# Slot packing and the slot-softmax multiply on GpSimd, and another order of the first loads, in a fused attention and maxout-FFN kernel

## The chip, the cores and the metric

The kernel runs on one core of a Trainium2 chip. The metric is device time in microseconds of one execution; lower is better. A profiled execution gives a trace of every instruction on the engines: TensorE (PE in the profile, its weight loads PEld), VectorE (DVE), ScalarE (ACT), GpSimd (POOL) and SyncE (SP), and of the DMA transfers.

## The reference

Eight batches of eight heads, 576 tokens, head size 64, 32 memory slots; then an FFN over the 4608 tokens with model size 512 and inner size 768.

```python
def _attn_ref(q, k, v, phi):
    a = phi - np.max(phi, axis=2, keepdims=True)
    a = np.exp(a)
    a = a / (np.sum(a, axis=2, keepdims=True) + 1e-09)      # over the tokens
    k_m = np.einsum('bhsm,bhsd->bhmd', a, k)                # slot keys
    v_m = np.einsum('bhsm,bhsd->bhmd', a, v)                # slot values
    scores = 1.0 / np.sqrt(q.shape[-1]) * np.matmul(q, k_m.transpose(0, 1, 3, 2))
    scores = scores - np.max(scores, axis=-1, keepdims=True)
    attn = np.exp(scores)
    attn = attn / (np.sum(attn, axis=-1, keepdims=True) + 1e-09)   # over the slots
    return np.matmul(attn, v_m)

def _moe_ref(x, w1, w2, w3, w_out):       # x: the heads side by side, [4608, 512]
    h = np.maximum(np.maximum(x @ w1, x @ w2), x @ w3)
    return h @ w_out
```

All inputs and the output are float32 in memory.

## The kernel before

**Order.** Nothing is scheduled by the framework (`tc.manual_schedule()`). The kernel ends in one long written list of words such as `B@2`, each a step of one batch, and `issue` turns a word into instructions. Every engine executes its own instructions in the order of this list, and waits where data or a buffer is missing. A `!` swaps the engine that evicts a result from PSUM (ScalarE or VectorE, by the table `EVAC`).

**Loads.** Loads that convert to bf16 are issued from GpSimd's queue: `load_kv` (k and v), `load_q`, `load_w` (w1, w2, w3) and `load_wo` (w_out); phi, which stays float32, goes from SyncE's queue for batch 0 and from GpSimd's for the others. In the list, `H0` and `H2` are the two halves of k of batch 0, `H1` and `H3` the two halves of v, `L0` to `L3` are phi, k, v and q, `Y0` to `Y3` are w1, w2, w3 and w_out. Inputs have two buffers each; `kvos` are two tiles with three parts for k, v and ones, the ones written once by VectorE at the start.

**Attention of a batch.** `E` takes the exponential of phi on ScalarE. `B` (`att_kv`, matmul at L209) multiplies it with k, v and the ones: 72 small multiplies, eight of them side by side in the array, each with 192 columns (64 of k, 64 of v, 64 ones, of which one column is the sum over the tokens). For batch 1 it is done in two parts, `B0` (k and ones) and `B1` (v). `N` divides by that sum on VectorE, `K` transposes the result by TensorE. `Q` transposes q on VectorE, `S` forms the scores and their exponentials e2. The softmax over the slots is done on VectorE with 32x32 transposes: `a` (L310) transposes e2 to t, `s` (L318) sums over the slots, `c` (L327) takes the reciprocals, `m` (`att_mul`, L332) multiplies, `X` (`att_back`, L340) transposes back into attn. Each of these five exists for two groups g = 0 and 1 of heads.

**FFN.** The slot values are multiplied into the weights, so that the FFN runs on attn directly: `D` (`fold`, L363) forms, for a batch, the product of v_m with w1 - w3 and w2 - w3 (`D0`, `D1`, `D2`, `D4`) and with w3·w_out (`D3`). The max of three products is written as w3 plus a max of differences; w3·w_out is formed once at the start (`W` transposes w3, `O0` to `O3` multiply with w_out at L161), and `V` (`w_diff`, L182) subtracts w3 from w1 and w2 in place. Batch 0 is folded before that subtraction, with a second term (`kvtn`), in four groups of columns given by `FIRST`. `F` (`ffn1`, L389) multiplies attn with a folded weight: the even ones take w1 and are evicted with a relu to h1, the odd ones take w2 and end in the max at L402 on VectorE (hT). `T` (`ffn2`, L420, L429, L438 and at the end L461, L469) forms 128 rows of the output, evicts them (L141) and stores them from SyncE's queue.

**PSUM** is used through one pool of four tiles, each for any step. `Z` issues multiplies of zeros that keep TensorE running at the start.

The steps around the change at the start stand in the list as

```
H3@0 I@0 H2@0 H0@0 H1@0 E@0 Z38@0 B@0 N@0 Z3@0 K@0 L3@0 Q0@0 Q1@0 Z7@0 S@0 a0@0 Y2@0
Y3@0 a1@0 s0@0 s1@0 c1@0 Z6@0 W0@0 W2@0 Y0@0 Y1@0 W1@0 Z10@0 O1@0 O0@0 O2@0 m1@0 D1@0!
c0@0 m0@0 X0@0 D0@0 O3@0 L0@1 L1@1 L3@1 L2@1 X1@0 F8@0 F0@0 V0@0 F2@0 D4@0! D2@0 L0@2
V2@0 F10@0 F6@0 F11@0 F9@0 E@1 F4@0 F3@0 F1@0 F7@0 F5@0 D3@0 B0@1 T3@0 N0@1 Q0@1 K0@1!
```

and the functions that the change touches are these:

Of the kernel before, what the change touches and what calls it, by code (L numbers as in the profile page):

```python
# [15 lines left out]
def kernel(  # L16
# [102 lines left out]
    warm = const.tile([P, BANK], BF16, name="warm")  # L119
    nc.vector.memset(warm, 0.0)  # L120
    nc.vector.memset(kvos[0][:, 2], 1.0)
    nc.vector.memset(kvos[1][:, 2], 1.0)

    def warm_up(n):
# [44 lines left out]

    w12 = w_sb[:, :, 0:2].rearrange("p j i f -> p j (i f)")  # L170

    FIRST = {0: (0, 384), 1: (384, 768), 2: (768, 1152), 4: (1152, 1536)}

    def columns(b, n):
        return FIRST[n] if b == 0 else (n * BANK, (n + 1) * BANK)

    def w_diff(n):

        c, end = n * BANK, (n + 1) * BANK
        while c < end:  # L180
# [6 lines left out]
            )  # L187
            c = e

    st = {}  # L190

    def att_exp(b, js=slice(0, NP)):
        s = st.setdefault(b, {})
        if "e" not in s:
            s["e"] = work.tile([P, NP, NC, M], BF16, name="e")
        nc.scalar.activation(out=s["e"][:, js], in_=loaded[b]["ph"][:, js], func=AF.Exp)  # L196

    def att_kv(b, part=None):
        s = st[b]
        kvp = acc_pool.tile([P, NG, BANK], FP32, name="kvp", tag="acc")  # L200
        s["kvp", part] = kvp
        kv = loaded[b]["kv"]
        cols = {None: slice(0, 3), 0: slice(0, 3, 2), 1: slice(1, 2)}[part]
        nd = {None: 3 * D, 0: 2 * D, 1: D}[part]
        for c in range(NC):
            for j in range(NP):
                for a in range(NG):
                    r = slice(HP * a, HP * (a + 1))
                    nc.tensor.matmul(  # L209
                        kvp[M * j : M * (j + 1), a, 0:nd],  # L210
                        lhsT=s["e"][r, j, c, :],
                        rhs=kv[r, cols, j, c, :],
                        start=(c == 0),
                        stop=(c == NC - 1),
                        tile_position=(HP * a, M * j),
                    )
# [57 lines left out]
    attns = {}  # L274

    def att_score(b):
# [22 lines left out]
        for a in range(NG):  # L299
# [4 lines left out]
                scale=0.125,  # L304
            )

    def att_t(b, g):
        s = st[b]
        t = s["t", g] = work.tile([P, S // HP, R, 2], BF16, name="t", tag=f"t{g}")
        nc.vector.transpose(  # L310
            out=t.rearrange("p n r e -> p (n r e)").bitcast(FP32),
            in_=s["e2"][:, g].bitcast(FP32),
        )
# [15 lines left out]
    def att_mul(b, g):  # L329
        s = st[b]  # L330
        t = s["t", g]
        nc.vector.tensor_tensor(  # L332
            out=t,
            in0=t,
            in1=s["sm", g].unsqueeze(2).to_broadcast([P, S // HP, R, 2]),
            op=ALU.mult,
        )

    def att_back(b, g):
        nc.vector.transpose(  # L340
            out=attns[b // 2][:, g, (b % 2) * S : (b % 2 + 1) * S].bitcast(FP32),
            in_=st[b]["t", g].rearrange("p n r e -> p (n r e)").bitcast(FP32),
        )
# [140 lines left out]
    def issue(b, n, swap):  # L484

        i = int(n[1:]) if len(n) > 1 else None
        {
            "I": lambda: make_identity(nc, ident),
            "Y": lambda: load_w(i) if i < 3 else load_wo(),
            "L": lambda: load_ph(b) if i == 0 else load_q(b) if i == 3 else load_kv(b, i - 1),  # L490
            "H": lambda: load_kv(b, i % 2, halves[i // 2]),
            "E": lambda: [att_exp(b, h) for h in (halves if b == 0 else [slice(0, NP)])],
            "B": lambda: att_kv(b, i),
            "N": lambda: att_kv_norm(b, i),
            "K": lambda: att_kv_t(b, swap, i),
            "Q": lambda: att_q(b, i),
            "S": lambda: att_score(b),
            "a": lambda: att_t(b, i),
            "s": lambda: att_sum(b, i),
            "c": lambda: att_rec(b, i),  # L500
            "m": lambda: att_mul(b, i),
            "X": lambda: att_back(b, i),
            "D": lambda: fold(b, i, swap),
            "F": lambda: ffn1(b, i, swap),
            "T": lambda: ffn2(b, i, swap),
            "W": lambda: w3_t(i, swap),
            "O": lambda: w3_o(i, swap),
            "V": lambda: w_diff(i),
            "Z": lambda: warm_up(i),
        }[n[0]]()  # L510


    for w in """
        H3@0 I@0 H2@0 H0@0 H1@0 E@0 Z38@0 B@0 N@0 Z3@0 K@0 L3@0 Q0@0 Q1@0 Z7@0 S@0 a0@0 Y2@0
        Y3@0 a1@0 s0@0 s1@0 c1@0 Z6@0 W0@0 W2@0 Y0@0 Y1@0 W1@0 Z10@0 O1@0 O0@0 O2@0 m1@0 D1@0!
        c0@0 m0@0 X0@0 D0@0 O3@0 L0@1 L1@1 L3@1 L2@1 X1@0 F8@0 F0@0 V0@0 F2@0 D4@0! D2@0 L0@2
        V2@0 F10@0 F6@0 F11@0 F9@0 E@1 F4@0 F3@0 F1@0 F7@0 F5@0 D3@0 B0@1 T3@0 N0@1 Q0@1 K0@1!
        T1@0 Q1@1 S@1 V1@0 E@2 L1@2 B1@1 L0@3 N1@1 a0@1 a1@1 K1@1 T2@0! s0@1 s1@1 D0@1 c0@1
        D2@1 c1@1 m0@1 D1@1! m1@1 T0@0! L2@2 X0@1 X1@1 F4@1! F5@1 L3@2 L2@3 F10@1 L1@3 F11@1
        F8@1 F0@1 F2@1 F3@1 L3@3 F6@1 F9@1 F1@1 E@3 F7@1 B@2 D3@1 N@2 Q1@2 Q0@2 T3@1 K@2! T2@1!  # L520
        S@2 a0@2 T1@1 T0@1! L0@4 D0@2 s0@2 L2@4 D1@2! a1@2 c0@2 m0@2 s1@2 c1@2 m1@2 X1@2 T4@1!
        X0@2 D3@2 L1@4 B@3 L0@5 N@3 D2@2 F6@2! Q1@3 F10@2 F2@2 F8@2 Q0@3 K@3! F3@2 F0@2 F7@2
        S@3 F1@2 F11@2 F4@2 F9@2 F5@2 E@4 D0@3 L1@5 a1@3 a0@3 D1@3! T0@2! T1@2 s0@3 D3@3 s1@3
        c1@3 m1@3 X1@3 D2@3 B@4 c0@3 E@5 T2@2! L2@5 L3@5 m0@3 X0@3 L3@4 F2@3 N@4 F0@3 F8@3
        F10@3 F1@3 F6@3 F3@3 K@4 F4@3 F7@3 F9@3 F5@3 D0@4 B@5 N@5 D1@4! F11@3 T3@2 Q0@5 K@5
        T4@3! Q1@5 S@5 L0@6 Q0@4 Q1@4 a1@5 a0@5 T1@3 s1@5 D0@5 S@4 T0@3! L0@7 s0@5 c0@5 a0@4
        c1@5 m0@5 D3@5 a1@4 m1@5 D1@5! D2@5 E@6 s1@4 X1@5 c1@4 T2@3! X0@5 s0@4 L2@7 T3@3 m1@4
        L1@7 F4@5 F0@5 F2@5 L3@7 c0@4 X1@4 m0@4 F1@5 F5@5 F3@5 X0@4 E@7 F10@5 F8@5 F9@5 D3@4
        B@7 N@7 D2@4 F11@5 F6@5 F4@4 F10@4 F8@4 Q0@7 L3@6 Q1@7 K@7 F7@5 L1@6 F0@4 Q1@6 S@7 a1@7
        L2@6 F11@4 s1@7 F5@4 a0@7 T1@5 s0@7 F6@4 c1@7 T3@5 c0@7 m0@7 F2@4 F1@4 F3@4 D1@7! D3@7  # L530
        B@6 m1@7 N@6 D2@7 T2@5! X1@7 Q0@6 K@6 F9@4 F7@4 S@6 T4@5! D0@7 a0@6 s0@6 X0@7 D0@6 a1@6
        s1@6 c1@6 m1@6 X1@6 T3@4 D3@6 D2@6 c0@6 D1@6! T0@5! T1@4 F6@7 F2@7 F0@7 m0@6 X0@6 F3@7
        F4@6 F8@6 F7@7 F9@6 F6@6 F2@6 F1@7 F5@6 F4@7 F5@7 F0@6 F7@6 F10@6 F8@7 F10@7 F9@7 F1@6
        F11@7 T2@4! F11@6 T2@7! F3@6 T1@7 T0@7! T2@6! T0@6! T3@6 T1@6 T0@4! T4@7! T3@7
    """.split():
        n, b = w.rstrip("!").split("@")
        issue(int(b), n, w.endswith("!"))
# [30 lines left out]
```

## Time and profile before

| | |
|---|---|
| median of 5 runs | 167.0 us (166.63 to 167.36) |
| the profiled execution | 167.07 us, its span 165.3 us |
| TensorE busy | 155.7 us, 94% of the span |
| VectorE, ScalarE, GpSimd busy | 104.6, 98.7, 28.3 us |
| granted TensorE clock | full in all 40 slices |
| DMA | 31.77 MB, mean 192 GB/s |

The profile is one execution. Its page gives the busy time of each engine, 40 equal slices of the span (a digit is the busy share in tenths), the chain of work that ended last, and groups of instructions by source line with their mean duration and the idle time ahead of them with what ended it. The trace also answers questions by time: a timeline of one engine, the busy time of a stretch, the landing time of each transfer (the time from its issue until its data is there). Busy time of GpSimd here counts the issue of loads, of which there are 37.

### The profile page before, as it was taken

What the parts mean: (1) busy time and instruction counts of PE and PEld (TensorE: products, weight loads), DVE (VectorE), ACT (ScalarE), POOL (GpSimd) and SP (SyncE); (2) the same over time, 40 slices, a digit from 0 to 9 for tenths busy, and PEclk for the clock granted to TensorE, in tenths of its full rate; (3) what the DMA queues carried; (4) which work ended last, traced back from release to release, by engine and by line L of the source; (5) the groups of instructions that cost most, each with busy time, mean ns of one, the idle gap of its engine ahead of it and who ended that gap; (6) DMA issues with size and microseconds to landing.
All of it is one profiled execution on the core that took longest, in us unless ns stands there. A gap on an engine that the chain in (4) does not pass through costs nothing.

```text
span 165.3 us, 4664 instructions
## 1 busy us (share of the span) xinstructions
PE 155.7 (94%) x2006; PEld 87.6 (53%) x2024; DVE 104.6 (63%) x196; ACT 98.7 (60%) x148; POOL 28.3 (17%) x43
## 2 busy tenths in 40 slices
PE   7998799999799999999999999999999999999990
PEld 2443434673367444755674437765544677544450
DVE  5406882597786766999399798979999076510010
ACT  4200216964598459997953899984859867124220
POOL 7952110050600500610104600000000000000000
PEclk9999999999999999999999999999999999999999
DMA  5999999999999999999999999993113200124342
GB/s 159 177 202 211 189 209 239 250 207 280 316 240 254 204 246 324 261 280 209 261 237 347 233 261 234 261 198 96 69 67 127 109 24 0 41 97 179 128 155 104
DMA packets 21973, 31.77 MB, mean 192 GB/s; under 512 B 1216, under 2 KB 16576, under 8 KB 21952
## 3 DMA queue, kind: packets, MB, share of 16 engines
q0 software_dynamic: 16080, 21.43, 67.5%
q1 hardware_dynamic: 5728, 9.90, 17.0%
q8 instruction: 16, 0.26, 0.6%
q10 hardware_dynamic: 144, 0.13, 0.2%
q14 instruction: 5, 0.04, 0.1%
HBM read 39.32 MB, written 9.44 MB: 295 GB/s over the span
## 4 chain that ended last, share of the span: by engine, by line
PE 83%; DMA 10%; POOL 3%; issue 2%; ACT 0%; DVE 0%; POOLq 0%; ACTq 0%
PE acc L389 29%; PE po L420 28%; DMA wo_sb<-in_moe_w_out_dram 10%; PE po L429 8%; PE wps L363 6%; PE kvp L209 4%; PE po L161 3%; POOL kvo L94 2%; PE sc L291 2%; PE po L438 1%; PE po L461 1%; PE kvtp L254 1%; POOL qq L102 0%; POOL w_sb L108 0%; PE po L469 0%
## 5 line engine op out<-in xcount | busy, mean ns | idle before, releaser
L420 PE MATMUL po<-wo_sb,hT 128*128 128x512 bf16 x195 | 50.4, 380 | 0.8
L389 PE MATMUL acc<-attn,wp 128*128 128x288 bf16 x384 | 50.2, 286 | 0.0
L402 DVE TENSOR_TENSOR hT<-acc,h 128x576 bf16<-128x576 f32 x48 | 34.4, 752 | 15.6 <-PE acc L389 10.1
L389 PEld LDWEIGHTS <-wp 128*128 128x128 bf16 x384 | 36.8, 98 | 12.4 <-issue 1.7
L141 ACT COPY ot<-po 128x512 f32<-128x512 f32 x35 | 20.6, 591 | 30.0 <-PE po L429 24.1
L141 ACT CAST wp<-wps 128x1024 bf16<-128x1024 f32 (+1 forms) x32 | 30.3, 1002 | 4.2 <-PE wps L363 4.2
L420 PEld LDWEIGHTS <-hT 128*128 128x128 bf16 x210 | 19.2, 98 | 23.5 <-issue 3.9
L139 ACT ACTIVATE h<-acc 128x576 bf16<-128x576 f32 x46 | 27.6, 663 | 4.5 <-PE acc L389 4.1
L429 PE MATMUL po<-wp,attn 128*128 128x512 bf16 x62 | 18.4, 379 | 0.0
L128 PE MATMUL po<-warm 128*128 128x512 bf16 x62 | 16.1, 416 | 1.4 <-DVE warm L120 1.2
L332 DVE TENSOR_TENSOR t<-t,sm 128x576 bf16<-128x576 bf16 x16 | 11.8, 745 | 0.3
L318 DVE TENSOR_REDUCE sm<-t 128x18 f32<-128x576 bf16 x16 | 11.5, 738 | 0.2
L269 DVE STREAM_TRANSPOSE qT<-qq 128x576 f32<-128x576 f32 x16 | 11.5, 752 | 0.0
L128 PEld LDWEIGHTS <-warm 128*128 128x128 bf16 x64 | 6.4, 105 | 9.3 <-issue 2.7
L300 ACT ACTIVATE e<-sc 128x576 bf16<-128x576 f32 x16 | 9.6, 654 | 2.9 <-PE sc L291 2.9
L310 DVE STREAM_TRANSPOSE t<-e 128x288 f32<-128x288 f32 x16 | 7.2, 464 | 6.2 <-ACT e L300 6.2
L94 POOL DMA_DIRECT2D kvo<-in_v_dram x9 | 6.8, 754 | 23.2 <-PE wps L363 14.3
L196 ACT ACTIVATE e<-ph 128x1152 bf16<-128x1152 f32 (+1 forms) x9 | 9.6, 1071 | 1.7 <-DMA ph<-in_phi_dram 1.7
L429 PEld LDWEIGHTS <-attn 128*128 128x128 bf16 x62 | 6.1, 98 | 7.3
L90 POOL DMA_DIRECT2D ph<-in_phi_dram x7 | 5.3, 764 | 25.0 <-ACT e L196 10.6
L209 PE MATMUL kvp<-kvo,e 64*32 64x192 bf16 (+2 forms) x648 | 8.3, 235 | 1.2 <-issue 0.9
L478 DVE COPY ot<-po 128x256 f32<-128x256 f32 x1 | 0.4, 425 | 14.2 <-PE po L469 14.2
(48 smaller groups left out, 108.5 us busy)
## 6 DMA issues: line engine op xcount, KB each, us to landing
out_dram<-ot SPq DMA_DIRECT2D x35, 256.0 KB, 5.5
qq<-in_q_dram POOLq DMA_DIRECT2D x8, 576.0 KB, 18.2
ph<-in_phi_dram POOLq DMA_DIRECT2D x7, 576.0 KB, 19.1
kvo<-in_k_dram POOLq DMA_DIRECT2D x7, 576.0 KB, 18.4
kvo<-in_v_dram POOLq DMA_DIRECT2D x7, 576.0 KB, 15.6
w_sb<-in_moe_w_dram POOLq DMA_DIRECT2D x3, 768.0 KB, 19.3
wo_sb<-in_moe_w_out_dram POOLq DMA_DIRECT2D x1, 768.0 KB, 16.4
ph<-in_phi_dram SPq DMA_DIRECT2D x2, 288.0 KB, 3.0
```

Of the source, the lines that this page charges most:

```text
L94: nc.gpsimd.dma_start(out=kv[:, i, h].rearrange("p j c d -> p j (c d)"), in_=by_pair((k, v)[i], b)[:, h],)
L128: nc.tensor.matmul(po[:, 0:BANK], lhsT=warm[:, 0:P], rhs=warm, start=True, stop=True)
L139: nc.scalar.activation(out=out_, in_=in_, func=AF.Relu)
L141: nc.scalar.copy(out=out_, in_=in_)
L209: nc.tensor.matmul(kvp[M * j : M * (j + 1), a, 0:nd], lhsT=s["e"][r, j, c, :], rhs=kv[r, cols, j, c, :], start=(c == 0), stop=(c == NC - 1 ...
L269: nc.vector.transpose(out=s["qT"][:, j].rearrange("p j c r e -> p (j c r e)").bitcast(FP32), in_=loaded[b]["q"][:, j].rearrange("p j c d - ...
L318: nc.vector.tensor_reduce(out=sm, in_=s["t", g].rearrange("p n r e -> p n e r"), op=ALU.add, axis=mybir.AxisListType.X,)
L332: nc.vector.tensor_tensor(out=t, in0=t, in1=s["sm", g].unsqueeze(2).to_broadcast([P, S // HP, R, 2]), op=ALU.mult,)
L389: nc.tensor.matmul(acc[:, h, 0:SH], lhsT=wps[b][:, g, w * DF + ft * P : w * DF + (ft + 1) * P], rhs=attn[:, g, c0 : c0 + SH], start=(g == ...
L402: nc.vector.tensor_tensor(out=hT[:, ft, (b % 2) * S : (b % 2 + 1) * S].rearrange("p (h n) -> p h n", h=2), in0=a, in1=s["h1", ft], op=ALU.max,
L420: nc.tensor.matmul(po, lhsT=hT[:, fc, c0 : c0 + P], rhs=wo_sb[:, fc, :], start=(n == 0), stop=False,)
L429: nc.tensor.matmul(po, lhsT=attn[:, g, c0 : c0 + P], rhs=wp3s[b][:, g, :], start=False, stop=(g == NG - 1),)
```

## The change

Five things change together.

1. *Packing.* From batch 2 on, a new step `r` copies k (`r0`) and v (`r1`) of a batch on GpSimd, in four copies each of 128 partitions x 576 elements, into a tile `kvr` in which k, v and a one of a token lie side by side. `B` then reads 129 columns in one piece instead of 192 in three.
2. *The multiply.* `m` (`att_mul`) runs on GpSimd instead of VectorE.
3. *The first loads.* Issued on GpSimd's queue in the order k, q, w3, w_out, v, w1, w2 instead of v, k, q, w3, w_out, w1, w2. Batch 0's `B` is done in two parts, the second after three of the w3·w_out blocks.
4. *Batch 0's softmax.* The sums over the slots come from a TensorE product with a block matrix of ones (`M`), the reciprocals from a logarithm and an exponential on ScalarE (`R`), and VectorE multiplies e2 with them; the transposes `a` and `X`, the sums and `m` are not used there. The column groups of batch 0's fold become 512, 256, 256 and 512.
5. *The written list* is a new one throughout.

```diff
+    kvrs = [
+        const.tile([P, NP, NC, 2 * D + 2], BF16, name=f"kvr{i}") for i in range(2)
+    ]
+    FULL = 2
+    def pack(b, i):
+        for j in range(NP):
+            nc.gpsimd.tensor_copy(
+                out=kvrs[b % 2][:, j, :, D * i : D * (i + 1)], in_=kvos[b % 2][:, i, j]
+            )
+    blkones = const.tile([P, P], BF16, name="blkones")
+    nc.vector.memset(blkones, 0.0)
+    for i in range(P // M):
+        nc.vector.memset(blkones[M * i : M * (i + 1), M * i : M * (i + 1)], 1.0)
-    FIRST = {0: (0, 384), 1: (384, 768), 2: (768, 1152), 4: (1152, 1536)}
+    FIRST = {0: (0, 512), 1: (512, 768), 2: (768, 1024), 4: (1024, 1536)}
+    ln = const.tile([P, S], FP32, name="ln")
+    ONES = {(0, 0), (0, 1)}
 def att_kv(b, part=None):
-        nd = {None: 3 * D, 0: 2 * D, 1: D}[part]
+        nd = {None: 3 * D if b < FULL else 2 * D + 1, 0: 2 * D, 1: D}[part]
+        kvr = kvrs[b % 2]
...
-                        rhs=kv[r, cols, j, c, :],
+                        rhs=kv[r, cols, j, c, :]
+                        if b < FULL
+                        else kvr[r, j, c, 0:nd],
+    def ones_sum(b, g):
+        sm = acc_pool.tile([P, 2, BANK], FP32, name="sm", tag="acc")
+        for h in range(2):
+            nc.tensor.matmul(
+                sm[:, h, 0:SH], lhsT=blkones,
+                rhs=e2[:, g, h * SH : (h + 1) * SH], start=True, stop=True,
+            )
+    def ones_rec(b, g):
+        nc.scalar.activation(
+            out=ln.rearrange("p (h n) -> p h n", h=2), in_=sm[:, :, 0:SH], func=AF.Ln,
+        )
+        r = work.tile([P, S], FP32, name="r")
+        nc.scalar.activation(out=r, in_=ln, func=AF.Exp, scale=-1.0)
+    def ones_mul(b, g):
+        nc.vector.tensor_tensor(
+            out=attns[b // 2][:, g, (b % 2) * S : (b % 2 + 1) * S],
+            in0=s["e2"][:, g, 0:S], in1=s["r", g], op=ALU.mult,
+        )
 def att_mul(b, g):
-        nc.vector.tensor_tensor(
+        nc.gpsimd.tensor_tensor(
 def issue(b, n, swap):
-            "I": lambda: make_identity(nc, ident),
+            "I": lambda: [make_identity(nc, ident)]
+            + [nc.gpsimd.memset(x[:, :, :, 2 * D : 2 * D + 1], 1.0) for x in kvrs],
+            "r": lambda: pack(b, i),
-            "X": lambda: att_back(b, i),
+            "X": lambda: (ones_mul if (b, i) in ONES else att_back)(b, i),
+            "M": lambda: ones_sum(b, i),
+            "R": lambda: ones_rec(b, i),
```

The new list, up to the scores of batch 3:

```
H0@0 H2@0 I@0 L3@0 Y2@0 E@0 Y3@0 Z25@0 B0@0 H3@0 N0@0 Z2@0 K0@0! H1@0 Q1@0 Q0@0 Z9@0
S@0 Z2@0 M0@0 R0@0 W2@0 M1@0 Y0@0 W0@0 Y1@0 L0@1 R1@0 X1@0 L1@1 X0@0 W1@0! Z7@0 O0@0
O2@0 O3@0 B1@0 N1@0 O1@0 K1@0 L3@1 D3@0 D1@0 D0@0 F8@0 V0@0 F10@0 F0@0 F6@0! F2@0 L2@1
D2@0 L1@2 V1@0 D4@0 F4@0 F1@0 F3@0 F11@0 L2@2 F5@0 E@1 F9@0 F7@0 B0@1 N0@1 L0@2 L3@2
T3@0 K0@1! T1@0 Q0@1 Q1@1 S@1 V2@0 a0@1 T0@0! a1@1 B1@1 s0@1 N1@1 c0@1 K1@1 s1@1 c1@1
D1@1! D0@1! D2@1 T2@0! m0@1 X0@1 D3@1 m1@1 L1@3 X1@1 F6@1 F2@1! F3@1 F8@1 F10@1 F9@1
F4@1 E@2 F11@1 r0@2 L2@3 F5@1 F0@1 F7@1 F1@1 r1@2 B@2 T2@1! L3@3 N@2 Q1@2 K@2 L0@3 Q0@2
T4@1! S@2 a0@2 T3@1 L2@4 D1@2! r0@3 s0@2 D0@2 c0@2 D2@2 a1@2 m0@2 s1@2 c1@2 T0@1! T1@1
m1@2 X0@2 X1@2 F0@2 L1@4 Q0@3 F6@2 L0@4 F2@2 Q1@3 F4@2 L3@4 F3@2 F5@2 E@3 F1@2 F8@2
D3@2 r1@3 B@3 N@3 L1@5 F9@2 F10@2 K@3 F7@2 F11@2 S@3 T0@2! L2@5 a1@3 D0@3 D3@3 T3@2
```

More of the change, by code (lines that the diff above doesn't have):

```diff
@@ L305, in att_score @@
             )
+    def ones_sum(b, g):
+        s = st[b]
+        e2 = s["e2"]
+        sm = acc_pool.tile([P, 2, BANK], FP32, name="sm", tag="acc")
+        for h in range(2):
+            nc.tensor.matmul(
+                sm[:, h, 0:SH],
+                lhsT=blkones,
+                rhs=e2[:, g, h * SH : (h + 1) * SH],
+                start=True,
+                stop=True,
+            )
+        s["sm", g] = sm
+    def ones_rec(b, g):
+        s = st[b]
+        sm = s["sm", g]
+        nc.scalar.activation(
+            out=ln.rearrange("p (h n) -> p h n", h=2),
+            in_=sm[:, :, 0:SH],
+            func=AF.Ln,
+        )
+        r = work.tile([P, S], FP32, name="r")
+        nc.scalar.activation(out=r, in_=ln, func=AF.Exp, scale=-1.0)
+        s["r", g] = r
+    def ones_mul(b, g):
+        s = st[b]
+        nc.vector.tensor_tensor(
+            out=attns[b // 2][:, g, (b % 2) * S : (b % 2 + 1) * S],
+            in0=s["e2"][:, g, 0:S],
+            in1=s["r", g],
+            op=ALU.mult,
+        )
     def att_t(b, g):
@@ L513 @@
     for w in """
[L514 to L531, printed above, removed]
@@ L532 @@
-        s1@6 c1@6 m1@6 X1@6 T3@4 D3@6 D2@6 c0@6 D1@6! T0@5! T1@4 F6@7 F2@7 F0@7 m0@6 X0@6 F3@7
-        F4@6 F8@6 F7@7 F9@6 F6@6 F2@6 F1@7 F5@6 F4@7 F5@7 F0@6 F7@6 F10@6 F8@7 F10@7 F9@7 F1@6
-        F11@7 T2@4! F11@6 T2@7! F3@6 T1@7 T0@7! T2@6! T0@6! T3@6 T1@6 T0@4! T4@7! T3@7
+        H0@0 H2@0 I@0 L3@0 Y2@0 E@0 Y3@0 Z25@0 B0@0 H3@0 N0@0 Z2@0 K0@0! H1@0 Q1@0 Q0@0 Z9@0
+        S@0 Z2@0 M0@0 R0@0 W2@0 M1@0 Y0@0 W0@0 Y1@0 L0@1 R1@0 X1@0 L1@1 X0@0 W1@0! Z7@0 O0@0
+        O2@0 O3@0 B1@0 N1@0 O1@0 K1@0 L3@1 D3@0 D1@0 D0@0 F8@0 V0@0 F10@0 F0@0 F6@0! F2@0 L2@1
@@ new lines @@
+        D3@2 r1@3 B@3 N@3 L1@5 F9@2 F10@2 K@3 F7@2 F11@2 S@3 T0@2! L2@5 a1@3 D0@3 D3@3 T3@2
+        r1@4 E@4 s1@3 L0@5 T2@2! a0@3 D1@3! s0@3 c1@3 D2@3 r0@4 B@4 m1@3 c0@3 T1@2 m0@3 X0@3
+        Q0@4 X1@3 F10@3 N@4 F0@3 L3@5 F6@3 Q1@4 K@4 L0@6 F4@3 F7@3 F1@3 r0@5 F5@3 F2@3 F3@3
+        F8@3 F11@3 F9@3 L2@6 S@4 E@5 r1@5 a0@4 T3@3 a1@4 s1@4 D0@4 D3@4 T4@3! c1@4 s0@4 c0@4
+        Q1@5 L1@6 D2@4 m1@4 B@5 D1@4! m0@4 Q0@5 X1@4 X0@4 T1@3 F6@4 N@5 L0@7 L3@6 F2@4 K@5 F3@4
+        F8@4 S@5 F7@4 a1@5 r1@6 F10@4 E@6 s1@5 F11@4 a0@5 L2@7 D1@5! D3@5 s0@5 T2@3! F9@4 c0@5
@@ new lines @@
+        c1@5 L1@7 F4@4 r0@6 F5@4 F0@4 F1@4 B@6 m0@5 X0@5 E@7 m1@5 N@6 D0@5 L3@7 D2@5 X1@5 Q1@6
+        T0@4! Q0@6 r1@7 K@6 F8@5 F2@5 F6@5 F9@5 F0@5 F3@5 r0@7 F4@5 F7@5 S@6 a0@6 F10@5 s0@6
+        F11@5 F1@5 F5@5 T0@3! D3@6 c0@6 D0@6 B@7 N@7 T3@5 m0@6 Q1@7 K@7 a1@6 Q0@7 X0@6 s1@6
+        T4@5! S@7 T2@4! a0@7 a1@7 s0@7 s1@7 D3@7 c0@7 D2@7 D0@7 T3@4 T2@5! c1@6 c1@7 m1@6 D1@6!
+        D1@7! X1@6 D2@6 m1@7 X1@7 T1@4 F4@6 m0@7 X0@7 T1@5 F8@7 F9@7 F2@6 F3@6 F2@7 F0@6 F6@6
+        F5@6 F0@7 F1@6 F7@6 F10@7 F3@7 F6@7 F8@6 F11@7 F1@7 F4@7 F5@7 F9@6 F10@6 F7@7 F11@6
@@ L535 @@
+        T0@7! T0@6! T2@7! T1@7 T0@5! T1@6 T2@6! T3@6 T4@7! T3@7
     """.split():
```

## The prediction

> **What bounds the kernel now.** I read the page first (busy shares, then the slices), then the chain of waits, then the landing times of the loads, then the timeline of VectorE for one batch.
>
> ```profile
> span 165.3 us, 4664 instructions
> PE 155.7 (94%) x2006; PEld 87.6 (53%) x2024; DVE 104.6 (63%) x196; ACT 98.7 (60%) x148; POOL 28.3 (17%) x43
> ...
> PEclk9999999999999999999999999999999999999999
> DMA  5999999999999999999999999993113200124342
> ...
> 6.21 16.35 DMA wo_sb<-in_moe_w_out_dram
> 22.56 0.14 issue
> 22.70 3.40 PE po L161 x15
> 26.10 0.05 issue
> 26.15 0.59 PE po L161 x2
> 26.74 0.77 PE wps L363 x32
> 27.52 1.40 PE po L161 x6
> 28.92 1.47 PE acc L389 x12
> ```
>
> The reader should see two stages. From 22.7 us to the end TensorE carries the chain: between 22.70 and 161.20 it is busy 136.32 of 138.50 us (view of busy time by stretches), so at most 2.2 us of idle TensorE can be won there. Before 22.7 the chain is one wait for w_out; TensorE runs idle multiplies by then. Time can come only from an earlier start of useful TensorE work, from less of it, or from those 2.2 us. VectorE at 63% is not the bound, so taking work off it wins nothing by itself. The DMA slices stay at 9 up to 111 us: the loads, too, run without a pause, only a little ahead of their use.
>
> The landing times (the issue on GpSimd's queue in the timeline plus the time to landing) give the order of the front:
>
> ```profile
> kvo<-in_v_dram POOLq DMA_DIRECT2D x1, 288.0 KB, 7.6
> qq<-in_q_dram POOLq DMA_DIRECT2D x1, 576.0 KB, 9.8
> w_sb<-in_moe_w_dram POOLq DMA_DIRECT2D x1, 768.0 KB, 13.3
> wo_sb<-in_moe_w_out_dram POOLq DMA_DIRECT2D x1, 768.0 KB, 16.4
> w_sb<-in_moe_w_dram POOLq DMA_DIRECT2D x1, 768.0 KB, 19.3
> ```
>
> Issued at 4.02, 4.73, 5.48, 6.21 and 7.02 us, they land at 11.65 (last half of v), 14.5 (q), 18.8 (w3), 22.6 (w_out) and 26.35 us (w1); w2 lands at 30.1. One after another: about 3 us for a whole k, q or v, 3.8 to 4.3 for a weight.
>
> The rows that price the change:
>
> ```profile
> L332 DVE TENSOR_TENSOR t<-t,sm 128x576 bf16<-128x576 bf16 x16 | 11.8, 745 | 0.3
> masks.py:199 POOL TENSOR_SCALAR_AFFINE_SELECT ident<-ident 128x128 bf16<-128x128 bf16 x1 | 0.3, 287 | 0.1
> masks.py:197 POOL MEMSET ident<- 128x128 bf16 x1 | 0.2, 228 | 0.0
> L552 POOL MEMSET const-float32-1.0<- 128x1 f32 x1 | 0.1, 98 | 0.0
> ...
> L209 PE MATMUL kvp<-kvo,e 64*32 64x192 bf16 x504 | 6.6, 243 | 0.3 <-DMA kvo<-in_v_dram 0.3
> ```
>
> L332 is the multiply that moves; the three GpSimd rows are all that this trace knows of GpSimd arithmetic.
>
> **Part 1, the order of the loads.** All nine first loads (k and v in halves, q, four weights) stay on GpSimd's queue at about 0.75 us an issue, and they are issued by some 8 us both times, long before they land; phi on SP's queue is unchanged. Two memsets of 36 elements each (about 0.13 us, from the memset rows) stand between them and cost nothing there. The two halves of v go behind w_out. So w_out lands 3 us sooner, at 19.6; v at 22.6; w1 and w2 have the same bytes ahead of them and stay at 26.35 and 30.1. TensorE can then do between 19.6 and 26.4 all four w3·w_out blocks (4 x 1.40), the v half of batch 0's slot product (72 small multiplies, 0.65), one transpose and the fold D3: 5.6 + 0.65 + 0.1 + 0.34 = 6.7 us, just filling the gap. Before, one block (1.40) and D3 (0.34) ran after w1. That is 1.74 won. Given back: D3 waits for the last block's eviction (0.59 on ScalarE), so D1 starts near 26.9 instead of 26.7; and F8 follows D1 and D0 directly, while before a w3·w_out block stood between, so it waits for D1's eviction, about 0.3. Net 1.2 to 1.3.
>
> **Part 2, 129 columns instead of 192** in six batches. Passes of 72 multiplies take 0.74 us at 192 columns and 0.64 at 128 in the chain; the passes at 64 are no shorter, so a floor is reached. 6 x 0.1 = 0.6 won, all on the path.
>
> **Part 3, batch 0.** Four ones products, four activations of about 0.65 us and two VectorE multiplies lie before 19.6, under the wait for w_out; the activations are of the set loaded at L62. Its k and q now land by about 8.8 and 11.7, so this cover is wide; without it, the two serial multiplies alone would cost 1.5. The regrouped fold columns total the same 1536. Cost 0.
>
> **Part 4, the multiply on GpSimd.** Fourteen instructions. From the trace: 0.098 + 576 x 1.02 ns (memset slope) = 0.69 at least; the affine select's slope, 1.49 ns, gives 0.95. Against them stands a rule of the Trainium skill, "GPSIMD Engine Reference", Engine selection: elementwise work with two inputs is about twice as slow on GpSimd as on VectorE and should stay there. On the 745 ns of L332 the ratio 1.96 of its section Performance versus the Vector engine makes 1.46 us. No GpSimd row here reads two tensors, so I take 1.46; range 0.95 to 2.0. What it costs is not 14 x 0.7, but what the later X delays. In batch 1: S ends near 39.4 instead of 40.7 (parts 1 and 2), then the reciprocal c0 at about 43.0, m0 to 44.5, m1 to 45.9, X1 to 46.4. TensorE, having done T2 and D3, reaches the first F of batch 1 at 46.0: a stall of 0.4 to 0.5. With 0.95 us there is none. X waits at the head of VectorE's queue, with the hT maxima of L402 behind it; so the same 0.5 is what they lose. In batch 2 the order leaves T3, three folds, T0 and T1 (5.8 us) after S, and the chain of about 5.8 just fits: 0.
>
> A second rule speaks against it: "SBUF — State Buffer" (section SBUF: two separate sides) says that GpSimd and a VectorE instruction with two SBUF inputs exclude each other for the whole instruction. The frequent VectorE row after the change, L402, reads one input from PSUM:
>
> ```profile
> L402 DVE TENSOR_TENSOR hT<-acc,h 128x576 bf16<-128x576 f32 x48 | 34.4, 752 | 15.6 <-PE acc L389 10.1 <-ACT h L139 5.2
> ```
>
> If it were blocked too, 12 per batch behind 8 copies of 0.7 could lose several us; I take 0, because the two-SBUF-input work left, L182 and batch 0's products, ends before the first GpSimd multiply.
>
> **Part 5, the packs, which decide.** Eight copies per batch from batch 2 on, 48 in all, each 576 elements. Price: 0.69 by the memset slope, 0.95 by the affine select's; a copy reads as well as writes, but does no comparison. I take 0.69, the nearest in work; range 0.55 to 0.95. They queue in order with the multiplies and with every load. For batch 2: m1 ends at 45.9; the k load of batch 3 (0.75), four copies, a v load (0.75), four copies: 45.9 + 1.5 + 5.5 = 52.9. TensorE reaches B of batch 2 at 46.4 + 12 x 0.495 = 52.4. Stall 0.5; each 0.1 us on a copy adds 0.8. In batch 3, after m1, three loads and four copies end at about 68.2 where TensorE arrives at 68.1: 0.1. After that the folds and T blocks leave room at 0.69. Data of batch 2 is there: by the same bytes as before, k lands at about 43.5, v at 47.3, phi at 49.1, q at 52.5. Loads queued behind the waiting GpSimd do not starve: while it waits for c0, four are outstanding to 52.5.
>
> **Sum.** -1.3 (part 1) - 0.6 (part 2) + 0.5 (part 4) + 0.6 (part 5) = -0.8. The profiled execution took 167.07 us (span 165.3 and 1.77 around it), 0.07 over the median of 167.0; 0.8 off the median is 166.2. The idle of 0.9 us ahead of kvp (put down to issue at 40.9 us, after 16 of its 72 multiplies, with v landed at 40.2) I keep.
>
> **The rivals.** *Slower: the packs are the bound.* At 0.80 a copy the stalls are 0.5 + 1.4 (B of batch 2) + 0.6 (B of batch 3) + 0.7 (first F of batch 3, since the multiplies wait behind packs) = 3.2, so 167.0 - 1.9 + 3.2 = 168.3; at 0.95 the same walk gives 6.2 and 171.3. It decides from about 0.73. For it: the affine select's row. Against it: the memset's. *All of it hides:* copies at or below 0.6 and multiplies near 1: 167.0 - 1.9 = 165.1, and 164.2 with the idle of 0.9 us gone too; 164.7 in the middle. For it: GpSimd is busy 17%. *The front wins nothing:* D1 still waits for w1, and the maxima of batch 0 on VectorE, busy from 31 to 37 us, set the pace: 166.2 + 1.3 = 167.5. For it: VectorE 4.96 of 5 us in 35 to 40. *The moved multiply does not do what it says*, since VectorE just waits in X: that lies inside the first.
>
> **How the numbers follow.** My forecast 0.40 (its own range 165.4 to 166.9), packs slow 0.35, all hides 0.15, front wins nothing 0.10. A measurement tells 0.3%, 0.5 us, from no change. Faster by more: 0.33 of the forecast and 0.15, 0.48; within: 0.07 and 0.05, 0.12; slower: 0.35 and 0.05, 0.40. The range runs from 164.5 to 169.4; it leaves out the worst of the slow packs (0.14) and the best end (0.04).
>
> **What would show it.** Right: w_out lands near 19.6, D1 starts by 26.9 with D3 before it; slot passes near 0.64; copies at 0.69 and multiplies near 1.46; TensorE idle before B of batch 2 and the first F of batch 1 about 0.5 each. Wrong: copies above 0.73, TensorE waiting for kvr in several batches; or L402 longer than 752 ns; or slices of DMA below 9 ahead of 100 us, which would mean loads held up in GpSimd's queue.

## The result and the profile after

The changed kernel takes 165.9 us (median of 28 runs, 165.18 to 167.40) against 167.07 us (47 runs): ratio 0.9939, 95% interval 0.9924 to 0.9953, so 1.0 us shorter (the two medians as they stand differ by 1.2). The forecast was 166.2 us, 0.8 us shorter, and the case held likeliest came. How the 1.0 us comes about is another matter: the gain forecast for the front and the stalls forecast behind it were each off by about 1.1 us.

The page of the changed kernel (span, busy time, slices):

```profile
span 164.3 us, 4836 instructions
PE 152.8 (93%) x2061; PEld 85.4 (52%) x2081; DVE 93.8 (57%) x181; ACT 101.3 (62%) x151; POOL 73.9 (45%) x107
...
PEclk9999999999999999999999999999999999999999
DMA  5999999999999999999999999994131330014333
```

GpSimd went from 28.3 to 73.9 us of busy time, VectorE from 104.6 to 93.8, and TensorE is as full as before (93% of the span against 94%). The clock row shows 9, that is 90% or more, in every slice of both. The loads end no earlier, near 111 us. The groups of instructions by line give the two new prices, and the maxima (L456, L402 before):

```profile
L105 POOL COPY kvr<-kvo 128x576 bf16<-128x576 bf16 x48 | 29.9, 672 | 8.6 <-DMA kvo<-in_v_dram 4.2 <-DMA kvo<-in_k_dram 2.6 <-PE acc L443 1.7
L386 POOL TENSOR_TENSOR t<-t,sm 128x576 bf16<-128x576 bf16 x14 | 16.0, 1152 | 26.7 <-DVE sm L381 26.7
L456 DVE TENSOR_TENSOR hT<-acc,h 128x576 bf16<-128x576 f32 x48 | 34.5, 753 | 14.1 <-PE acc L443 8.0 <-ACT h L153 5.8
```

The multiply takes 1.15 us where VectorE took 0.745, a copy 0.67, and four copies in a row 2.49, 0.62 from start to start. The idle before a multiply is its wait for the reciprocal on VectorE; the multiply is not late, its input is. The maxima take 753 ns, as before (752): GpSimd's work beside them does not slow them.

The chain of waits in the front (start, duration, what; pieces of 0.05 us and less are left out, "..." stands for more):

```profile
4.99 15.32 DMA wo_sb<-in_moe_w_out_dram
20.31 0.14 issue
20.45 4.04 PE po L175 x18
...
26.95 0.95 PE wps L417 x18
27.93 0.70 DVE wp L159
28.67 2.66 PE acc L443 x20
```

and the first F in the timeline of the kernel before:

```profile
28.75 1.63 PE L389 MATMUL acc<-attn,wp 128*128 128x288 bf16 x12
```

w_out lands at 20.3 instead of 22.6, and all four w3·w_out blocks and the multiplies of D3 are out by 27.3. But F begins at 28.67, where it began at 28.75 before. Of the 1.7 us of work moved ahead, the 1.4 that stood in front of F are nearly used up in between.

### The profile page after: what moved, and what is told of

The parts are those of the page before. It is cut to its first block, busy times and chain, and to the rows that moved or that the text cites. A ratio compares the mean times of both kernels' runs of the same rounds, so it can differ in the third digit from the quotient of the medians.

```text
span 164.3 us, 4836 instructions
## 1 busy us (share of the span) xinstructions
PE 152.8 (93%) x2061; PEld 85.4 (52%) x2081; DVE 93.8 (57%) x181; ACT 101.3 (62%) x151; POOL 73.9 (45%) x107
## 4 chain that ended last, share of the span: by engine, by line
PE 81%; DMA 9%; issue 2%; POOL 2%; DVE 2%; ACT 1%; ACTq 0%; POOLq 0%
PE po L474 28%; PE acc L443 27%; DMA wo_sb<-in_moe_w_out_dram 9%; PE po L483 8%; PE wps L417 6%; PE kvp L226 4%; PE po L175 3%; PE sc L310 1%; PE po L492 1%; PE kvtp L273 1%; PE po L515 1%; POOL kvo L98 1%; ACT h L153 1%; DVE hT L456 0%; POOL w_sb L118 0%
## 5 line engine op out<-in xcount | busy, mean ns | idle before, releaser
L456 DVE TENSOR_TENSOR hT<-acc,h 128x576 bf16<-128x576 f32 x48 | 34.5, 753 | 14.1 <-PE acc L443 8.0
L105 POOL COPY kvr<-kvo 128x576 bf16<-128x576 bf16 x48 | 29.9, 672 | 8.6 <-DMA kvo<-in_v_dram 4.2
L153 ACT ACTIVATE h<-acc 128x576 bf16<-128x576 f32 x46 | 28.5, 659 | 7.8 <-PE acc L443 6.8
L155 ACT CAST wp<-wps 128x1024 bf16<-128x1024 f32 (+1 forms) x31 | 29.5, 1015 | 1.8 <-PE wps L417 1.8
L386 POOL TENSOR_TENSOR t<-t,sm 128x576 bf16<-128x576 bf16 x14 | 16.0, 1152 | 26.7 <-DVE sm L381 26.7
L142 PE MATMUL po<-warm 128*128 128x512 bf16 x43 | 11.7, 418 | 1.4 <-DVE warm L130 1.2
L372 DVE TENSOR_REDUCE sm<-t 128x18 f32<-128x576 bf16 x14 | 10.3, 738 | 0.3
L394 DVE STREAM_TRANSPOSE attn<-t 128x288 f32<-128x288 f32 x14 | 6.2, 456 | 5.6 <-POOL t L386 5.6
L364 DVE STREAM_TRANSPOSE t<-e 128x288 f32<-128x288 f32 x14 | 6.6, 471 | 5.0 <-ACT e L319 4.8
L112 POOL DMA_DIRECT2D qq<-in_q_dram x8 | 6.1, 762 | 7.1 <-DMA w_sb<-in_moe_w_dram 7.1
```

The costliest lines, as they stand in the source:

```text
L105: nc.gpsimd.tensor_copy(out=kvrs[b % 2][:, j, :, D * i : D * (i + 1)], in_=kvos[b % 2][:, i, j])
L142: nc.tensor.matmul(po[:, 0:BANK], lhsT=warm[:, 0:P], rhs=warm, start=True, stop=True)
L153: nc.scalar.activation(out=out_, in_=in_, func=AF.Relu)
L155: nc.scalar.copy(out=out_, in_=in_)
L372: nc.vector.tensor_reduce(out=sm, in_=s["t", g].rearrange("p n r e -> p n e r"), op=ALU.add, axis=mybir.AxisListType.X,)
L386: nc.gpsimd.tensor_tensor(out=t, in0=t, in1=s["sm", g].unsqueeze(2).to_broadcast([P, S // HP, R, 2]), op=ALU.mult,)
```

## The experiments

Each ratio is against the kernel before, in runs interleaved on one chip; "longer than the changed kernel" is the difference of two such ratios times 167.

**e1, v of batch 0 loaded ahead of q, w3 and w_out**

```diff
-        H0@0 H2@0 I@0 L3@0 Y2@0 E@0 Y3@0 Z25@0 B0@0 H3@0 N0@0 Z2@0 K0@0! H1@0 Q1@0 ...
+        H0@0 H2@0 H3@0 H1@0 I@0 L3@0 Y2@0 E@0 Y3@0 Z25@0 B0@0 N0@0 Z2@0 K0@0! Q1@0 ...
```

> The changed kernel with one thing undone: both halves of v of batch 0 are issued right behind k, ahead of q, w3 and w_out, as in the kernel before. Everything else stays, the w3·w_out blocks ahead of the folds too. Theory A (the order of the loads is worth what lets the four w3·w_out blocks run while w1 is still under way): w_out lands 2.8 to 3 us later, near 23.2 instead of 20.3, the four blocks end near 28.8 and D1 starts near 30 instead of 27.3; the kernel gets 2.5 us longer than the changed one, 168.4, slower than the kernel before by about 0.8%. Rival B (the front is paced by the maxima on VectorE and by w2 anyway): less than 0.7 us longer, 166.6 or under.

169.03 us, ratio 1.0121 (1.0086 to 1.0155), 3.0 us longer than the changed kernel. Theory A. The timeline of TensorE shows the blocks starting 3.1 us later:

```profile
23.59 4.05 PE L175 MATMUL po<-wo_sb,w3T 128*128 128x512 bf16 x18
```

**e8, D3 moved so that it covers D1's eviction, and the evictions of O1 and K1 swapped**

```diff
-        O2@0 O3@0 B1@0 N1@0 O1@0 K1@0 L3@1 D3@0 D1@0 D0@0 F8@0 ...
+        O2@0 O3@0 B1@0 N1@0 O1@0! K1@0! L3@1 D1@0 D0@0 D3@0 F8@0 ...
```

> The changed kernel with the fold D3 of batch 0 moved behind D1 and D0, and the evictions of O1 and K1 swapped between ScalarE and VectorE, so that D1 waits neither for the last w3·w_out block nor for its eviction, and D3 covers D1's eviction. Theory A (0.65 us of idle TensorE at 26.3 and 0.4 at 28.3 are what the front lost against the prediction): up to 0.7 us shorter than the changed kernel, 165.2, faster than both. Rival B (behind the front the maxima on VectorE pace batch 0, and give nothing on): within 0.2 us.

165.93 us, ratio 0.9952 (0.9934 to 0.9971): not told apart from the changed kernel. Rival B by the time, though not by its reason. Timelines of TensorE and ScalarE:

```profile
20.09 4.04 PE L175 MATMUL po<-wo_sb,w3T 128*128 128x512 bf16 x18 [0.69 <-DMA wo_sb<-in_moe_w_out_dram]
...
27.61 1.93 ACT L155 CAST wp<-wps 128x1024 bf16<-128x1024 f32 x2 [0.86 <-PE wps L417]
27.93 2.87 PE L443 MATMUL acc<-attn,wp 128*128 128x288 bf16 x20 [0.17 <-DVE wp L159]
29.42 2.30 ACT L153 ACTIVATE h<-acc 128x576 bf16<-128x576 f32 x4
31.23 0.41 PE L417 MATMUL wps<-w_sb,kvt 64*32 64x512 bf16 x8
```

Counted from the start of the w3·w_out blocks, the first fold comes at 6.53 us (6.50 in the changed kernel, where it is D3; its D1 comes at 6.82), F at 7.84 instead of 8.22, and B0 of batch 1 at 15.23 instead of 15.15 us. The 0.4 us won at F is gone at D4 already, which comes at 11.14 us (31.23 in the timeline) instead of 11.04, before the first maximum on VectorE (12.96 instead of 12.87). So the maxima did not take it. The trace points to ScalarE: it evicts two folds and then four F without a pause, there are four PSUM tiles, and D4 begins 0.05 us behind the end of the third of those four, at 31.18. No run tests this by itself.

**e9, batch 0's softmax without the ones product**

```diff
-    ONES = {(0, 0), (0, 1)}
+    ONES = set()
-            "M": lambda: ones_sum(b, i),
-            "R": lambda: ones_rec(b, i),
+            "M": lambda: [att_t(b, i), att_sum(b, i)],
+            "R": lambda: [att_rec(b, i), att_mul(b, i)],
```

(with batch 0's multiply on VectorE)

> The changed kernel without the ones product in batch 0: its softmax over the slots is done as in the other batches (two transposes, sum, reciprocal and multiply for each group, all on VectorE, some 5.3 us of it instead of 1.5), at the same places of the list. Theory A (the prediction's zero: all of it lies under the wait for w_out, from 14 to 20 us): within 0.3 us of the changed kernel, 165.6 to 166.2. Rival B (VectorE is then late with the evictions of w3's transposes, and the w3·w_out blocks start late): 1 us or more longer, 167.

165.82 us, ratio 0.9952 (0.9928 to 0.9975). Theory A: the ones product is worth nothing that can be seen here.

**e2, the multiply back on VectorE**

```diff
-        nc.gpsimd.tensor_tensor(
+        nc.vector.tensor_tensor(
```

> The changed kernel with the multiply of the slot softmax back on VectorE, 0.745 instead of 1.15 us, and nothing else changed. Theory A (VectorE is not the bound; the multiply is worth nothing where it stands): within 0.3 us of the changed kernel, 165.6 to 166.2. Rival B (VectorE's relief is where the gain comes from, since the maxima wait in its queue): 0.5 us or more longer, 166.4 and up. Rival C (the slower multiply costs by its chain): 0.3 to 0.6 us shorter than the changed kernel.

169.21 us, ratio 1.0135 (1.0105 to 1.0165): 3.3 us longer than the changed kernel. Rival B, which said 0.5 us or more. The chain of waits shows where to look:

```profile
44.63 1.08 DVE wp L159
45.71 0.67 DVE t L386
...
92.92 1.30 DVE t L386 x2
...
106.28 0.68 DVE t L386
```

The chain that ends last leaves TensorE and runs along VectorE from 43.4 to 48.1 us, from 89.8 to 96.6 and from 105.5 to 111.4; the multiplies at L386 stand in all three, between transposes, sums and evictions that need the same engine. In the changed kernel the chain stays with TensorE there, but for 0.9 us at 43 and 3.0 us at 94.5 (waits put down to issue counted in).

To stand in the chain is not yet to cost. Counted by the starts of S in the two timelines, 1.3 us are lost between the S of batches 1 and 2, 0.4 between those of 4 and 5, 1.6 between those of 5 and 6, and nothing elsewhere: 3.3 in all. The first loss is seen at F of batch 1: after two multiplies it waits for VectorE's transpose at L394 and goes on 8.3 us after S, where the changed kernel begins F 6.9 us after S. The new list has also given VectorE the eviction of D0 of batch 1 (`D0@1!`, 1.08 us in the chain), which was ScalarE's in the old one. What part that has in the loss was not tested.

**e3, no packs (192 columns read from kvo in every batch)**

```diff
-    FULL = 2
+    FULL = B
-            "r": lambda: pack(b, i),
+            "r": lambda: None,
```

> The changed kernel without the packs: the slot product reads k, v and the 64 ones in 192 columns in every batch, and GpSimd copies nothing. Theory A (129 columns are worth 0.05 to 0.1 us a batch, and the packs cost nothing): 0.4 to 0.6 us longer than the changed kernel, 166.4. Rival B (the packs cost as much as they win, by stalls ahead of the slot product or by holding up loads): within 0.2 us of it, or shorter.

166.52 us, ratio 0.9977 (0.9955 to 0.9999): 0.6 us longer than the changed kernel, whose interval it just clears. Theory A. In the timelines a pass of 192 columns takes 0.93 us (six of six), one of 129 takes 0.80 to 0.83: 0.7 us in six batches.

**e4, both**

> The changed kernel with both: no packs (192 columns) and the multiply on VectorE, so that GpSimd only issues loads. What is left of the change is the order of the first loads, batch 0's ones product and the written list. Theory A (the two GpSimd parts are worth 0.5 us together): 166.4, still 0.5 us under the kernel before, which is then the part of the front and the list. Rival B (all of the gain is GpSimd's work): 167.0 or more.

168.84 us, ratio 1.0100 (1.0079 to 1.0122). Not theory A; it lies in rival B's range, but the list without GpSimd's work does not come out level with the kernel before, as B would have it: it is 1.7 us slower. From e2 this run differs in the packs (and with them in the columns), so in whether GpSimd copies while VectorE multiplies; their times are not told apart. The durations are (shortest/median/longest in ns), e2 first:

```profile
L386 DVE TENSOR_TENSOR t<-t,sm x14: 715/750/1087, 45.6 to 129.5; 128x576 bf16<-128x576 bf16 x14
L105 POOL COPY kvr<-kvo x48: 661/674/1251, 43.8 to 112.6; 128x576 bf16<-128x576 bf16 x48
```

e4, and the copies of the changed kernel:

```profile
L386 DVE TENSOR_TENSOR t<-t,sm x14: 712/742/759, 45.2 to 129.0; 128x576 bf16<-128x576 bf16 x14
L105 POOL COPY kvr<-kvo x48: 657/670/700, 47.0 to 112.6; 128x576 bf16<-128x576 bf16 x48
```

The mean of a multiply rises from 736 to 782 ns, but the mean hides what happens. Two of e2's 14 multiplies, those at 61.69 and 107.39 us, begin in the middle of a copy and take 0.98 and 1.09 us; the others take 0.76 at most. Three of the 48 copies, at 45.65, 61.97 and 107.81, meet a multiply that is under way and take 1.20 to 1.25; the others 0.70 at most. That agrees with the Trainium skill, "SBUF — State Buffer" (section SBUF: two separate sides): of a GpSimd instruction that reads SBUF and a VectorE instruction with two inputs there, the second waits until the first is through. It was rare here, 0.6 us for all 14 multiplies.

**e10, the same move of the multiply in the kernel before**

```diff
-        nc.vector.tensor_tensor(
+        (nc.vector if b == 0 else nc.gpsimd).tensor_tensor(
```

> The kernel before, its list untouched, with the multiply of the slot softmax on GpSimd from batch 1 on (batch 0's stays on VectorE). The run with the multiply moved back showed 3.2 us for it in the new list. Theory A (a matter of the list: the old one has set enough TensorE work against VectorE's chain, so relief gains nothing, and the slower multiply with loads queued behind it costs): within 0.5 us of the kernel before or slower. Rival B (VectorE's relief is worth some us in any list): 1 us or more shorter, 166.0 or under.

175.18 us, ratio 1.0489 (1.0447 to 1.0531), 8.2 us longer than the kernel before. Theory A, and worse than it said. Its waits, a piece of GpSimd's timeline and the DMA slices:

```profile
POOL t L332 <- DVE sm L327: 65.9, 7, 16.8
PE kvp L209 <- DMA kvo<-in_k_dram: 4.4, 1, 4.4
...
98.11 2.27 POOL L332 TENSOR_TENSOR t<-t,sm 128x576 bf16<-128x576 bf16 x2 [14.05 <-DVE sm L327]
...
102.67 0.81 POOL L94 DMA_DIRECT2D kvo<-in_k_dram  x1
...
DMA  5999999999689999999999379999303130033433
```

The same load of k, of batch 7, in the kernel before:

```profile
87.94 0.76 POOL L94 DMA_DIRECT2D kvo<-in_k_dram  x1 [0.38 <-issue]
```

The loads stand behind multiplies in GpSimd's queue, and a multiply waits up to 16.8 us for its sum. This k goes out 14.7 us later than before, and TensorE waits 4.4 us for it. The DMA slices fall to 6, 8, 3 and 7 where they were 9, and DMA holds 29% of the chain instead of 10%. By the starts of S, 6.2 us are lost between batches 4 and 7, where this wait stands; what makes up the rest was not taken apart.

**e12 and e5, five and six copies in a pack instead of four**

```diff
-        for j in range(NP):
+        for j in [0, 0, 1, 2, 3]:        # e12; e5: [0, 0, 1, 1, 2, 3]
```

> The changed kernel with five copies in each pack instead of four, as if a copy took 0.78 us instead of 0.62. With six (0.93) the kernel took 5.9 us more than the changed one. Theory A (a threshold, the prediction's break-even near 0.73: the packs of batch 2 end near 53.9 against a slot product at 53.0): 1 to 2.5 us longer, 167 to 168.4. Rival B (no threshold, the loss is in proportion): 3 us, 168.9. Rival C (it is far from the edge, and six copies cost by holding up the loads): under 166.4.

> The changed kernel with six copies in each pack instead of four (the first two are made twice, into the same place), 12 a batch at 0.62 us from start to start: as if a copy took 0.93. The prediction's walk of GpSimd's queue: with multiplies of 1.15, the packs of batch 2 end 2.5 us later, near 55.1, against a slot product reached at 53.0: a stall of 2; then 1 to 2 more in batches 3 and 4: 169 to 170. Rival (GpSimd has room, 45% busy, and a late pack is made up for by PSUM and by the blocks behind it): under 167.

e12: 167.12 us, ratio 1.0021 (1.0000 to 1.0043), 1.4 us longer than the changed kernel. e5: 171.91 us, ratio 1.0267 (1.0222 to 1.0312), 5.5 us longer. In both what was expected came, theory A for e12 and the prediction's walk for e5: the fifth copy costs 1.4 us, the sixth 4.1 more, so there is a threshold just above the changed kernel's own load. In e12 the slot product of batch 2 meets copies that are not done (timeline of TensorE):

```profile
52.67 0.23 PE L226 MATMUL kvp<-kvr,e 64*32 64x129 bf16 x2 [0.31 <-POOL kvr L105]
53.28 0.75 PE L226 MATMUL kvp<-kvr,e 64*32 64x129 bf16 x66 [0.38 <-POOL kvr L105]
```

In e5 TensorE waits for copies in five places, 2.5 us in all (read from one execution, of 173.0 us).

**e6 and e7, the idle of 0.9 us in the slot product of batch 1**

```diff
 # e6, the kernel before
-        ... S@1 V1@0 E@2 L1@2 B1@1 L0@3 N1@1 a0@1 a1@1 K1@1 T2@0! s0@1 ...
+        ... S@1 V1@0 T2@0! E@2 L1@2 B1@1 L0@3 N1@1 a0@1 a1@1 K1@1 s0@1 ...
 # e7, the changed kernel
-        ... S@1 V2@0 a0@1 T0@0! a1@1 B1@1 s0@1 N1@1 c0@1 K1@1 ...
+        ... S@1 V2@0 a0@1 a1@1 B1@1 s0@1 N1@1 c0@1 T0@0! K1@1 ...
```

> The kernel before with one word moved: T2 of batch 0 (8 multiplies of 512 columns, 1.72 us) stands between S and B1 of batch 1 instead of behind them. Theory A (the 0.9 us idle in B1 is the fetch of TensorE's instructions: S and B1 are 32 and 72 pairs of weight load and multiply of some 10 ns each[...]): the idle is gone, and up to 0.9 us with it, 166.2 to 166.6. Rival B (the idle has to do with v of batch 1 or with the slot product itself): it stays in B1, or ahead of it, and the time is that of the kernel before.

> The changed kernel with T0 of batch 0 moved from between S and B1 of batch 1 to behind B1, so that the two bursts of small multiplies stand side by side as in the kernel before. Theory A (instruction fetch): an idle of 0.5 to 1 us put down to issue turns up inside or at the end of B1, while the wait of K1 for N1 (0.43) and for kvt (0.32) is covered by T0: the time within 0.3 us of the changed kernel. Rival B (v of batch 1, or nothing of this kind): no idle, and 0.5 to 0.8 us shorter.

e6: 167.59 us, ratio 1.0055 (1.0035 to 1.0074). The idle inside B1 is gone, as theory A said, and yet the time is 0.9 us longer than the kernel before, since two waits that T2 had covered now lie open (timeline of TensorE; the wait of 0.43 us ahead of K1 stands in both kernels):

```profile
44.16 0.84 PE L363 MATMUL wps<-w_sb,kvt 64*32 64x512 bf16 x24 [0.62 <-DVE kvt L145]
...
47.59 6.06 PE L389 MATMUL acc<-attn,wp 128*128 128x288 bf16 x48 [0.76 <-ACT wp L141]
```

e7: 166.15 us, ratio 0.9956 (0.9928 to 0.9984). No idle inside B1, but one ahead of it:

```profile
42.03 0.75 PE L226 MATMUL kvp<-kvo,e 64*32 64x64 bf16 x72 [1.75 <-DMA kvo<-in_v_dram]
```

v of batch 1 landed at 41.96 here, at 40.5 in the changed kernel's profile and at 40.2 in that of before. The profiled execution took 166.99 us, 0.8 more than the median of its kernel, so this wait need not stand in the others. So e7 could not test the fetch of instructions: the wait for v took its place. What the idle inside B1 was stays open. What is shown is that in the new list T0, standing there, covers it or the wait for v.

**e11, the eviction of D1 of batch 4 on VectorE instead of ScalarE (on top of e8)**

```diff
-        ... B@5 D1@4! m0@4 ...
+        ... B@5 D1@4 m0@4 ...
```

> The changed kernel with D3 of batch 0 moved as in the run before, and the eviction of D1 of batch 4 given to VectorE instead of ScalarE. In the changed kernel's chain 2 us near 95 us lie on ScalarE and VectorE: ScalarE's evictions run without a break from 90.2 to 94.5 and the output block evicted at 94.97 and two activations come late. Theory A (ScalarE's queue is what ends there): 0.5 to 1 us shorter than the changed kernel, 165.2. Rival B (VectorE takes over the lateness, as it is busy with X, Q and the maxima there): the same time or longer.

166.72 us, ratio 0.9987 (0.9960 to 1.0014), 0.8 us longer than the changed kernel and 0.6 longer than e8. Rival B: in its chain 92.1 to 94.8 us now lie on VectorE, and the eviction moved there is the first piece of them, 1.23 us. The wait has changed engines and is not undone. No version ran that beats the changed kernel.

## Why the prediction was right or wrong, point by point

**Part 1, the loads: the order right, the net size wrong.** w_out was forecast at 19.6 and landed at 20.3 (its blocks begin at 19.96 in e9, 20.09 in e8); w1 at 26.9 instead of 26.35. The order carries: e1 costs 3.0 us. The failed term is the net "1.2 to 1.3". S of batch 1, ahead of which both kernels do the same steps on TensorE but for the ones products, begins at 40.12 instead of 40.26: 0.14.

The block that no longer stands ahead of F was worth 1.30 us from start to start. Of that, 0.60 went because D1 came at 27.27 and not at 26.67 (0.2 was forecast), 0.24 because the folds D1 and D0 spread over 1.02 us instead of 0.78 (nothing was forecast), and 0.38 in the wait for D1's eviction (0.3 was forecast). That leaves 0.08 at F. D3, now ahead of F, should have given 0.2 to 0.3 more behind it; 0.06 is left of this at S. e8 took the last of the three waits away and won nothing, so something behind the front sets the pace; its trace points to ScalarE's evictions, which is not shown by a run of its own. In size this was the rival "the front wins nothing", which I gave 0.10; its reason, the maxima on VectorE, is not what the traces show.

**Part 2, the columns: right.** 0.6 forecast, 0.6 in e3. The floor that I read is not quite one: a pass of 64 columns takes 0.75 us, of 129 columns 0.80 to 0.83. And the columns change only from batch 2 on, so they could not bring S of batch 1 forward, as part 4 has it; its 1.3 us there is part 1 alone.

**Part 3, batch 0: right.** Zero forecast, zero in e9 within what the runs can tell.

**Part 4, the multiply: the price too high, the reading of its worth wrong.** I took 1.46 us from the ratio of 1.96 in the Trainium skill, "GPSIMD Engine Reference" (section Performance versus the Vector engine); measured 1.152, a ratio of 1.55. The stall of 0.5 us ahead of batch 1's first F did not come: F follows D3 without idle, at 47.04. The price is not the whole reason. Counted from the end of S, X1 was done after 6.2 us instead of the forecast 7.0, and 0.5 of this difference is an earlier reciprocal c0 (3.1 instead of 3.6). With 1.46 us a multiply and the measured reciprocals, X1 would have ended at about 47.2 (an estimate from the timeline), a stall of 0.2.

The step that failed is the sentence that VectorE is not the bound "so taking work off it wins nothing by itself", read in the old list and carried over to the new one. In the new list the multiply on VectorE costs 3.3 us (e2). There an engine at 62% of the span bounded stretches of 5 to 7 us. Why the new list is so much tighter for VectorE than the old one, which ran with the multiply there, is open; the added eviction is one candidate. The skill's rule that elementwise work belongs on VectorE (the same page, section Engine selection) would have kept the slower kernel here. In e10 following it is right by 8.2 us, and what the waits show there is the queue, loads held behind waiting multiplies, and not the ratio.

The second rule, on two instructions that exclude each other, I took at 0, and that was right: the maxima stayed at 753 ns and no copy of the changed kernel took more than 0.70 us. e2 shows what was avoided.

**Part 5, the packs: the walk right, the price a little high.** 0.69 us forecast for a copy, 0.62 from start to start. The second pack of batch 2 ended at 52.6, the slot product began at 53.05, and the 0.6 us of stalls did not come:

```profile
45.08 1.16 POOL L386 TENSOR_TENSOR t<-t,sm 128x576 bf16<-128x576 bf16 x1 [0.18 <-DVE sm L381]
46.18 0.80 POOL L98 DMA_DIRECT2D kvo<-in_k_dram  x1
46.98 2.49 POOL L105 COPY kvr<-kvo 128x576 bf16<-128x576 bf16 x4
49.42 0.74 POOL L98 DMA_DIRECT2D kvo<-in_v_dram  x1
50.15 2.48 POOL L105 COPY kvr<-kvo 128x576 bf16<-128x576 bf16 x4
```

These are the loads and copies that the walk of part 5 had written down, in its order, behind the second multiply. The threshold was placed at 0.73; at an effective 0.78 (e12) 1.4 us are lost and the kernel stands level with the one before, at 0.93 (e5) 5.5. That the price of a copy decides was right, and the threshold lay only 0.1 us from the measured 0.62.

**The idle that I kept: wrong.** The 0.9 us in B1 were to stay. They are gone, as T0 now stands between S and B1; e6 shows the same with another block. From S (L291, L310) to K1 (L254, L273), before:

```profile
40.26 0.47 PE L291 MATMUL sc<-qT,kvt 32*32 32x288 bf16 x32
...
41.81 0.61 PE L209 MATMUL kvp<-kvo,e 64*32 64x64 bf16 x56 [0.89 <-issue]
42.85 0.23 PE L254 MATMUL kvtp<-ident,kvn 128*128 128x128 bf16 x1 [0.43 <-DVE kvn L229]
```

and after:

```profile
40.12 0.48 PE L310 MATMUL sc<-qT,kvt 32*32 32x288 bf16 x32
...
43.55 0.23 PE L273 MATMUL kvtp<-ident,kvn 128*128 128x128 bf16 x1 [0.43 <-DVE kvn L248]
44.09 0.84 PE L417 MATMUL wps<-w_sb,kvt 64*32 64x512 bf16 x24 [0.32 <-DVE kvt L159]
```

Counted from S, K1 begins 3.43 us later instead of 2.59, with the 1.72 us of T0 done in between: 0.88 won, more than any other term. About 0.5 was given back behind K1: the folds begin 0.54 us after it, with a wait for kvt, where before T2 followed after 0.07. The wait ahead of K1 stands in both. That makes 0.4 net. e7, which moves T0 away again, is 0.3 longer than the changed kernel by its ratio; that cannot be told from nothing, nor from 0.4.

**The sum.** Forecast: -1.3 - 0.6 + 1.1 = -0.8. From the two traces: -0.14 in the front, -0.9 from the idle, +0.5 in the wait behind it, and from there to the end a remainder of -0.5, which the columns (-0.6) explain: -1.0. That the total came close is in good part luck: a front that was too large and stalls that were too large had opposite signs, and an idle that I did not count made up the rest.

The single undos add up to 3.0 + 3.3 + 0.6 = 6.9 us, for a change worth 1.0; the last two together (e4) cost 2.7 and not 3.9. A list written for all parts together loses with each part taken out; what the list itself costs or wins cannot be read from them.

## What to carry to other kernels

The worth of moving work to another engine is read from the stretches where the first engine is the chain, not from its share of the span, and from what stands in the second engine's queue behind the moved instruction. How much such a stretch costs is read from how late the same step begins in two traces: 6.8 us in the chain cost 0.4 in e2. A load queued behind an instruction that waits is held up with it: the same multiply was worth 3.3 us in a list whose DMA slices stayed at 9, and cost 8.2 in one where they fell to 3. A mean can hide a collision; look at the longest of a group. Where a walk of a queue leaves 0.1 us per instruction to the threshold, test the threshold on the chip with one instruction more.

## What the runs showed of the hardware that was not expected

GpSimd's multiply of a bf16 and a float32 input, 576 elements, takes 1.15 us, 1.55 times VectorE's; its copy of 576 bf16 elements repeats every 0.62 us. VectorE's multiply with two SBUF inputs and such a copy excluded each other where they met in e2: multiplies of 0.98 and 1.09 us instead of 0.75, copies of 1.20 to 1.25 instead of 0.67. VectorE's maxima with one input in PSUM stayed at 753 ns. A whole pass of 72 small multiplies falls from 0.93 to 0.81 us from 192 to 129 columns, a third fewer columns for an eighth less time.
